# Zeros in the padded columns of two kinds of exponential tiles, written by ScalarE in place of GpSimd

## The chip, the core and the metric

The kernel runs on one core of a Trainium2 chip. The metric is the device time of one execution in microseconds (us). The core's engines are named as the profile names them: PE (TensorE, with PEld for its weight loads), DVE (VectorE), ACT (ScalarE), POOL (GpSimd) and SP (SyncE, which issues the large transfers). Each engine takes its instructions from its own queue, in the order in which the program wrote them.

## The reference, cut to what matters

An induced attention is followed by a soft mixture of experts, all in float32.

```python
def mab(q, kv):                       # B, N, m, C = 4, 11456, 32, 128
    s = scale * (q @ kv.transpose(0, 2, 1))
    s = s - s.max(-1, keepdims=True)
    a = np.exp(s)
    a /= a.sum(-1, keepdims=True) + 1e-09
    return a @ kv
h = mab(I, x)                         # 32 inducing points attend to x
x = mab(x, h).reshape(B * N, C)       # x attends to them
logits = x @ phi                      # 45824 x 32 slots
d = np.exp(logits - logits.max(0, keepdims=True))
d /= d.sum(0, keepdims=True) + 1e-9
slot_input = (d.T @ x).reshape(E, S_per_e, D)     # E, S_per_e, D = 8, 4, 128
slot_out[e] = np.maximum(slot_input[e] @ w1[e], 0.0) @ w2[e]   # hidden size 1024
c = np.exp(logits - logits.max(1, keepdims=True))
c /= c.sum(1, keepdims=True) + 1e-9
return c @ slot_out
```

## The kernel before, in words

Each of the 4 batches has 11456 rows of x, laid out as 90 blocks of 128 rows. A batch is cut into 6 tiles, five of 16 blocks and one of 10, so there are 24 tiles, and 12 pairs of them. Scores are kept as 32 rows (inducing points or slots) by four groups of 32 rows of x per block. In the last block of a batch only 64 rows are real. In the turned layout this leaves 16 columns of padding at the end of each batch's last tile: `valid(n)` is `width(n) - 16` there.

Stages, for each batch: the tiles of x are loaded (`xn`, and for most a transposed copy `xt`); the scores against the inducing points are formed pair by pair (`s`), their running maximum is taken, ACT writes the exponentials into `et` (L357, with a sum of the row), they are transposed (L369 on DVE, or L378 on PE with a copy back) and multiplied with `xn` (L393). After a batch's three pairs `group_fin` forms h. Then for each tile of that batch (`group_b`) follow the second attention (`s2p`, `bt`, `a`) and the logits (`lp`, kept in `l_all`). Three tiles make a segment (`group_seg`): the maximum over the segment (L780, L788, L791), the exponentials `dt` of its three tiles (L802, with the row sums in `z_l`), their transposes `d` (L808 on DVE, or PE and a copy), and the product with `a` into `u` (L818).

When all eight segments stand, `group_mlp` joins them: weights for the segments (`wl`, L864 and L903), the sum `zw` (L868), zeroed tiles `ma` and `mb` (g0: L952, and L954 twice), a matrix `wsel` of segment weights within `mb` (L877, POOL), its spreading over the partitions by PE (`wr`, L882), a weighted sum of the `u` (L885, L889, DVE), the expert inputs `sip` and `sit` (L894, L942), the last addition into `z1s` within `ma` (L957), the hidden layer (`hpm`, L967), its transposes (`htm` L980, with DVE copies L985), the second layer (`so`, L996) and its spreading (L1003, L1006, L1009). Fills (L231) are matmuls on zeros that keep PE at work. Then the outputs: each tile's row sums `zp` (L1106), the product `po` (L1125), evictions into `ot` by DVE, ACT or ACT with POOL (L1146, L1148, L1151, L1155), and stores (L1175). The softmax over slots for the outputs, the c-tiles, is done in between: maximum L1066 and its spreading L1070 on DVE, subtraction L1074 on POOL, exponential L1077 on ACT.

Every operation is recorded in a list with an engine, a cost and its dependences, and the list `ORDER` of operation numbers, written out by hand or by a planner beforehand, sets in which order they are issued. The costs given to `op` do not enter that order here; it stands in the code. Semaphore waits come from the buffers: `RINGS` gives `et` one buffer and `dt` two. The second buffer of `dt` that tile 23 takes was tile 21's before.

The padding of the exponentials has to be zero, since it is transposed and multiplied with the rest. The exponential writes the first `v` columns, and a second instruction, belonging to the same recorded operation, writes zeros to the other 16:

```python
nc.scalar.activation(et[:, :v], T["s1", p][:, :v], AF.Exp, ..., accum_out=zsum)   # L357
if v < w:
    nc.gpsimd.memset(et[:, v:w], 0.0)                                             # L359
```

The same is done for `dt` at L802 to L804. This happens for four pairs (2, 5, 8, 11) and four tiles (5, 11, 17, 23): eight memsets of 128x16 in all. `wz` (L226) is a constant 128x128 tile of zeros that DVE fills at the start and that the fills read.

Of the kernel before, what the change touches and what calls it, by code (L numbers as in the profile page):

```python
# [100 lines left out]
def width(n):  # L101
    return SIZES[n % NCH] * S


def seg_of(n):

    k = max(k for k in range(NSEG) if SEG_AT[k] <= n)
    return k, n - SEG_AT[k]
# [6 lines left out]
def valid(n):  # L115
    return width(n) - (PADS if n % NCH == NCH - 1 else 0)
# [24 lines left out]
class Plan:  # L141
# [6 lines left out]
    def op(self, eng, cost, name, fn, reads=(), writes=(), allocs=(), ni=0, uses=()):  # L148
        self.ops.append([eng, cost, name, fn, reads, writes, allocs, ni, uses])
# [3 lines left out]
def tile_kernel(ctx, tc, xn, xt_d, ind_t, phi, w1, w2, consts, out):  # L153
    nc = tc.nc
# [11 lines left out]
    def wtile(tag, key, n=JM * S):  # L166
        T[key] = work.tile([P, n], F32, tag=tag, name="_".join(map(str, key)), bufs=RINGS[tag])
        return T[key]

    def stile(tag, key, n=1, bufs=8):  # L170
        T[key] = small.tile([P, n], F32, tag=tag, name="_".join(map(str, key)), bufs=bufs)
        return T[key]

    def ptile(tag, key):
        T[key] = (pools[-1] if tag in ("sa", "sb") else ps).tile([P, 512], F32, tag=tag, name="_".join(map(str, key)), bufs=RINGS[tag])
        return T[key]
# [49 lines left out]
    wz = const.tile([P, P], F32, name="wz")  # L226
# [6 lines left out]
    def tiles_of(four):  # L233
        return [slice(32 * g, 32 * g + 32) for g in range(4)] if four else [slice(0, P)]

    def l_of(n):
        o = STARTS[n % NCH] * S
        return l_all[:, n // NCH, o : o + width(n)]

    def pe_turn(src_key, src, n, dst_tag, dst_key, prio, extra=(), virt=()):  # L240

        tk = ("tt", dst_key)
        dst = [(dst_tag, dst_key)]

        def tr():
            if virt:
                wtile(dst_tag, dst_key)
            pt = ptile("mm", tk)
            for q in range(4):
                nc.tensor.transpose(pt[:, q * P : (q + 1) * P], src()[:, q * P : (q + 1) * P], ident)  # L250

        def ev():
            nc.scalar.copy(T[dst_key] if virt else wtile(dst_tag, dst_key), T[tk])

        plan.op("PE", 0.48, prio, tr, [src_key, *extra], [tk], [("mm", tk), *((v, tk) for v in virt), *(dst if virt else ())], ni=8)
        plan.op("ACT", 0.48, prio, ev, [tk], [dst_key], [] if virt else dst)
# [59 lines left out]
    def group_pair(p):  # L316
# [3 lines left out]
        w, v = 512 + width(a1), 512 + valid(a1)  # L320

        def pr(op):
            return a1, op
# [29 lines left out]
        def aex():  # L353
            et = wtile("et", ("et", p), 1024)
            t = stile(hk[0], hk, P + 2, 2)
            zsum = T["hz", b][:, P + 1 :] if apart else t[:, P : P + 1]
            nc.scalar.activation(et[:, :v], T["s1", p][:, :v], AF.Exp, bias=T["negm1", b][:, c : c + 1], accum_out=zsum)  # L357
            if v < w:
                nc.gpsimd.memset(et[:, v:w], 0.0)  # L359

        def e_of(a):
            o = 512 * (a % 2)
# [46 lines left out]
        hk = ("hs", p) if c else ("hz", b)  # L409
# [8 lines left out]
        op = plan.op  # L418
        prev = [("ng", p - 1)] if c else []
        both = [("s1", a0), ("s1", a1)]  # L420
# [4 lines left out]
            op("ACT", 0.38 if c else 0.19, pr("am5"), am5, [("m1", p), *prev], [("m5", p)], [("m5", ("m5", p))])  # L425
        op("PE", 0.22, pr("apm"), apm, [("m5", p)], [("pm", p)], [("mm", ("pm", p))], ni=16 if p in CP else 4)
        op("DVE", 0.07, pr("ang"), ang, [("pm", p)], [("ng", p)])
        op("ACT", 0.24 + w / 1200, pr("aex"), aex, [*both, ("ng", p)], [("et", p), hk, ("zc", p)], [("et", ("et", p)), (hk[0], hk)], uses=[("s1", p)])
        if c:
            op("ACT", 0.19, pr("aal"), aal, [("ng", p), *prev], [("al", p)], [("al", ("al", p))])  # L430
            op("ACT" if p in HM else "Pool", 0.26 if p in HM else 0.4, pr("aal"), ahm, [("al", p)], [("hz", b)])
# [232 lines left out]
    def a2_of(n):  # L664
        return T["a2", n][:, : width(n)]
# [93 lines left out]
    def negm_of(k):  # L759

        k += k == NSEG - 1
        return negm_l[:, k : k + 1]

    def group_seg(k):
        op = plan.op
        seg = SEGS[k]
        ns = range(SEG_AT[k], SEG_AT[k] + seg)
        b = ns[0] // NCH
        last = ns[-1]

        def pr(o, n=last):
            return n, "B", o

        def h1():
            m4 = stile("m4b", ("m4b", k), SEG * 4)[:, : seg * 4]
            if HS[k] == "A":
                for i in range(seg):
                    nc.scalar.mul(m4[:, 4 * i : 4 * i + 4], mask4, T["mx2", k][:, i : i + 1])
                return
            (nc.vector if HS[k] == "D" else nc.gpsimd).tensor_tensor(  # L780
                m4.rearrange("p (i g) -> p i g", g=4), T["mx2", k][:, :seg].unsqueeze(2).broadcast_to([P, seg, 4]),
                mask4.unsqueeze(1).broadcast_to([P, seg, 4]), op=ALU.mult,
            )

        def h2():
            pmb = ptile("mm", ("pmb", k))
            for r in tiles_of(k in CH):
                nc.tensor.matmul(pmb[r, : seg * 4], rep[:, r], T["m4b", k][:, : seg * 4], start=True, stop=True)  # L788

        def h3():  # L790
            nc.vector.tensor_reduce(negm_of(k), T["pmb", k][:, : seg * 4], axis=AX.X, op=ALU.max, negate=True)  # L791

        op({"D": "DVE", "A": "ACT", "P": "Pool"}[HS[k]], {"D": 0.08, "A": 0.19 * seg, "P": 0.25}[HS[k]], pr("bch"), h1, [("mx2", n) for n in ns], [("m4b", k)], [("m4b", ("m4b", k))])
        op("PE", 0.22, pr("bch"), h2, [("m4b", k)], [("pmb", k)], [("mm", ("pmb", k))], ni=16 if k in CH else 4)
        op("DVE", 0.08, pr("bch"), h3, [("pmb", k)], [("ngl", k)])

        for i, n in enumerate(ns):

            def de(n=n, i=i):
                v = valid(n)  # L800
                dt_ = wtile("dt", ("dt", n))
                nc.scalar.activation(dt_[:, :v], l_of(n)[:, :v], AF.Exp, bias=negm_of(k), accum_out=z_l[:, k, i : i + 1])  # L802
                if v < width(n):
                    nc.gpsimd.memset(dt_[:, v : width(n)], 0.0)  # L804

            def td(n=n):
                w = width(n)
                nc.vector.transpose(wtile("d", ("d", n))[:, :w], T["dt", n][:, :w])  # L808

            def c2(n=n, i=i):  # L810

                if i == 0:
                    ptile("u", ("u", k))
                u, a2, d, nb = T["u", k], a2_of(n), T["d", n], SIZES[n % NCH]
                for j in range(nb):
                    q = slice(32 * (j % 4), 32 * (j % 4) + 32)
                    c = slice(j * S, j * S + S)
                    nc.tensor.matmul(u[q, :S], a2[:, c], d[:, c], start=i == 0 and j < 4, stop=i == seg - 1 and j >= nb - 4)  # L818

            w = width(n)  # L820
            op("ACT", 0.28 + w / 1200, pr("bde"), de, [("l", n), ("ngl", k)], [("dt", n), ("z", n)], [("dt", ("dt", n))])
            if n in TB:
                pe_turn(("dt", n), lambda n=n: T["dt", n], n, "d", ("d", n), pr("btd"))
            else:
                op("DVE", 0.07 + w / 960, pr("btd"), td, [("dt", n)], [("d", n)], [("d", ("d", n))])
            op("PE", 0.02 + 0.28 * w / 512, pr("c2"), c2, [("d", n), ("a2", n)], [("u", k)], [("u", ("u", k))] if i == 0 else [], ni=w // 8)

        if k < NSEG - 1:

            def u1():  # L830
                nc.scalar.copy(us_all[:, k * S : (k + 1) * S], T["u", k][:, :S])

            op("ACT", 0.16, pr("uf"), u1, [("u", k)], [("us", k)])
# [367 lines left out]
    for a in range(NT):  # L1201
        group_a(a)
        if a % 2:
            group_pair(a // 2)
        if a % NCH == NCH - 1:
            b = a // NCH
            group_fin(b)
            for n in range(b * NCH, (b + 1) * NCH):
                group_b(n)
                k, i = seg_of(n)  # L1210
                if i == SEGS[k] - 1:
                    group_seg(k)
# [89 lines left out]
```

## Time and profile before

| | |
|---|---|
| time, median of 3 runs | 228.7 us (228.14 to 229.79) |
| the profiled execution's own time | 228.22 us |
| its span in the profile | 226.4 us |
| mean granted clock of TensorE | 0.959 |
| PE / DVE busy | 202.7 us (90%) / 175.8 us (78%) |
| POOL / ACT busy | 130.3 us (58%) / 128.0 us (57%) |
| moved by DMA | 75.01 MB, mean 331 GB/s |

Times in the rows are microseconds from the start of the span. A busy PE is one whose pipeline holds matmuls; its ends are modelled. The granted clock is a share of 2.4 GHz. A row of a timeline gives start, duration, engine, line, operation, output and inputs, and in brackets how long the engine was idle before it and which instruction ended that.

### The profile page before, as it was taken

How to read it: one execution, taken by the hardware profiler on the slowest of the kernel's cores; microseconds unless marked ns; L12 is line 12 of the kernel's file. 1: busy time of each engine (PE TensorE's matmuls, PEld its weight loads, DVE VectorE, ACT ScalarE, POOL GpSimd, SP SyncE). 2: the span in 40 equal slices, each digit the busy share in tenths (PEclk: the TensorE clock that was granted, in tenths of full speed). 3: DMA queues.
4: the chain of work that ended last, by engine and by line, in shares of the span. 5: the costliest groups of instructions: out<-in, count | busy, mean ns of one | idle time of the engine just before them, and what ended most of it. 6: DMA issues, size and time to landing. Idle time of an engine off the chain costs nothing.

```text
span 226.4 us, 8096 instructions
## 1 busy us (share of the span) xinstructions
PE 202.7 (90%) x3370; PEld 141.9 (63%) x3370; DVE 175.8 (78%) x410; ACT 128.0 (57%) x339; POOL 130.3 (58%) x170
## 2 busy tenths in 40 slices
PE   8887899999999999999999998699999999899820
PEld 8664563546454663556654686598888878787710
DVE  0065548899899999999999998478898989868520
ACT  2463344563356676567764775133386699866730
POOL 0000105694537897588889982834669696867530
PEclk9999999999999999999999999659999999999975
DMA  6999998999999999999999900000099999999992
GB/s 225 402 428 417 428 420 323 377 427 419 400 376 389 414 388 360 410 389 419 387 412 427 395 14 0 3 3 3 28 408 403 403 395 419 393 421 421 404 408 89
DMA packets 14004, 75.01 MB, mean 331 GB/s; under 512 B 1808, under 2 KB 2448, under 8 KB 6928
## 3 DMA queue, kind: packets, MB, share of 16 engines
q1 hardware_dynamic: 13536, 74.32, 81.0%
q8 instruction: 26, 0.43, 0.7%
q10 hardware_dynamic: 432, 0.18, 0.3%
q14 instruction: 10, 0.08, 0.1%
HBM read 50.91 MB, written 23.59 MB: 329 GB/s over the span
## 4 chain that ended last, share of the span: by engine, by line
PE 55%; DVE 14%; DMA 13%; ACT 6%; issue 5%; POOL 3%; POOLq 0%; SPq 0%; ACTq 0%; DVEq 0%
PE po L1125 8%; PE zp L1106 7%; PE s L462 6%; DMA xt<-xt 5%; DMA xn<-xn 5%; PE ha L393 5%; PE s2p L462 4%; PE lp L715 4%; DMA l_all<-xt 3%; PE warm L231 2%; PE hpm L967 2%; DVE m L326 2%; PE u L818 2%; PE tp L290 2%; DVE bm L578 2%
## 5 line engine op out<-in xcount | busy, mean ns | idle before, releaser
L1155 POOL TENSOR_TENSOR ot<-ot,rzo 128x512 f32<-128x512 f32 (+1 forms) x26 | 25.9, 1006 | 15.6 <-ACT ot L1148 13.7
L1074 POOL TENSOR_TENSOR cs<-l_all,cs 128x512 f32<-128x512 f32 (+1 forms) x24 | 28.7, 1206 | 9.1 <-DVE cs L1070 9.1
L1125 PE MATMUL po<-mb,l_all 32*128 32x128 f32 x704 | 29.8, 285 | 1.7 <-ACT ot L1151 0.7
L1146 DVE TENSOR_TENSOR ot<-po,rzo 128x512 f32<-128x512 f32 (+1 forms) x48 | 28.3, 622 | 1.7 <-PE po L1125 1.4
L1151 ACT ACTIVATE ot<-po,rzo 128x128 f32<-128x128 f32 x85 | 24.1, 380 | 8.5 <-PE po L1125 7.2
L600 POOL TENSOR_TENSOR bt<-bt,bm 128x512 f32<-128x512 f32 (+1 forms) x21 | 20.6, 987 | 13.5 <-DVE bm L578 12.0
L1125 PEld LDWEIGHTS po<-mb,l_all 32*128 32x128 f32 x704 | 24.6, 186 | 5.7 <-DVE ot L1146 1.2
L690 POOL TENSOR_TENSOR a<-bt,bz 128x512 f32<-128x512 f32 (+1 forms) x24 | 23.7, 994 | 5.6 <-DVE bz L626 3.8
L1106 PE MATMUL zp<-cst,l_all 128*128 128x128 f32 x176 | 25.9, 287 | 0.9 <-DVE rzo L1114 0.6
L1106 PEld LDWEIGHTS zp<-cst,l_all 128*128 128x128 f32 x176 | 21.5, 190 | 4.4 <-issue 1.2
L715 PE MATMUL lp<-a2t,bdg 128*128 128x512 f32 (+1 forms) x48 | 23.6, 594 | 0.0
L393 PE MATMUL ha<-xn,e 128*32 128x128 f32 x668 | 21.9, 274 | 0.4 <-DMA xn<-xn 0.4
L393 PEld LDWEIGHTS ha<-xn,e 128*32 128x32 f32 x668 | 18.2, 110 | 3.8 <-issue 1.7
L617 POOL TENSOR_TENSOR hbuf<-bt 128x256 f32<-128x256 f32 (+1 forms) x24 | 16.7, 698 | 6.7 <-ACT bt L609 6.6
L357 ACT ACTIVATE et<-s,negm 128x1024 f32<-128x1024 f32 (+1 forms) x12 | 12.7, 1057 | 13.8 <-DVE negm L351 13.0
L462 PE MATMUL s<-xt,it_sb 128*32 128x512 f32 (+1 forms) x152 | 18.1, 571 | 2.6 <-ACT et L357 1.5
L802 ACT ACTIVATE dt<-l_all,negm_l 128x512 f32<-128x512 f32 (+1 forms) x24 | 16.6, 693 | 5.6 <-DVE negm_l L791 4.3
L462 PE MATMUL s2p<-xt,hts 128*32 128x512 f32 (+1 forms) x152 | 18.4, 574 | 0.2 <-ACT hts L491 0.2
L1148 ACT COPY ot<-po 128x512 f32<-128x512 f32 (+1 forms) x26 | 14.4, 580 | 4.7 <-PE po L1129 1.9
L609 ACT ACTIVATE bt<-bt 128x512 f32<-128x512 f32 (+1 forms) x23 | 13.6, 600 | 5.3 <-POOL bt L600 3.1
L1077 ACT ACTIVATE l_all<-cs 128x512 f32<-128x512 f32 (+1 forms) x24 | 14.1, 616 | 4.0 <-POOL cs L1074 4.0
L326 DVE TENSOR_REDUCE m<-s 128x1 f32<-128x1024 f32 (+1 forms) x12 | 13.6, 1136 | 2.1 <-PE s L462 2.0
(187 smaller groups left out, 390.7 us busy)
## 6 DMA issues: line engine op xcount, KB each, us to landing
xn<-xn SPq DMA_DIRECT2D x18, 1024.0 KB, 11.3
xt<-xt SPq DMA_DIRECT2D x13, 1024.0 KB, 10.1
out<-ot SPq DMA_DIRECT2D x12, 1024.0 KB, 6.9
w<-w SPq DMA_DIRECT2D x8, 1024.0 KB, 9.8
out<-ot SPq DMA_DIRECT2D x10, 512.0 KB, 6.3
l_all<-xt SPq DMA_DIRECT2D x3, 1024.0 KB, 7.2
out<-ot SPq DMA_DIRECT2D x12, 256.0 KB, 2.9
xt<-xt SPq DMA_DIRECT2D x3, 640.0 KB, 10.3
```

Source lines behind the costliest of these rows:

```text
L326: nc.vector.tensor_reduce(stile("m1", ("m1", p)), T["s1", p][:, :v], axis=AX.X, op=ALU.max)
L393: nc.tensor.matmul(ha[32 * q : 32 * q + 32, :P], e[:, j * S : (j + 1) * S], T["xn", a][:, j * P : (j + 1) * P], start=a == a0 and j < 4, s ...
L462: nc.tensor.matmul(dst[32 * g : 32 * g + 32, :w], lhs, src, start=True, stop=True)
L600: nc.gpsimd.tensor_tensor(tv, tv, mb(), op=ALU.subtract)
L690: nc.gpsimd.tensor_tensor(blocks(a2), blocks(t), zb, op=ALU.mult)
L715: nc.tensor.matmul(lp[r, :w], T["bdg", b][:, r], T["a2t", n][:, :w], start=True, stop=True)
L1074: nc.gpsimd.tensor_tensor(t, l_of(n), t, op=ALU.subtract)
L1106: nc.tensor.matmul(zp[:, q * P : (q + 1) * P], e[:, q * P : (q + 1) * P], mask4s, start=True, stop=True, skip_group_check=True)
L1125: nc.tensor.matmul(T[po[g]][:, q * P : (q + 1) * P], e[r, q * P : (q + 1) * P], T["srs",][r, :], start=True, stop=True, skip_group_check=True)
L1146: nc.vector.tensor_tensor(dst, src, parts(g)[1], op=ALU.mult)
L1151: nc.scalar.mul(dst[:, q], src[:, q], T["rzo", n][:, g + 4 * q : g + 4 * q + 1])
L1155: nc.gpsimd.tensor_tensor(dst, dst, z, op=ALU.mult)
```

## The change

The two memsets are replaced by ACT copies of as many columns of `wz`. Two costs in the recorded operations are raised by 0.09 to account for them; the list `ORDER` is the same, so each copy stands in ACT's queue right behind the exponential whose tile it completes.

```diff
             nc.scalar.activation(et[:, :v], T["s1", p][:, :v], AF.Exp, bias=T["negm1", b][:, c : c + 1], accum_out=zsum)
             if v < w:
-                nc.gpsimd.memset(et[:, v:w], 0.0)
+                nc.scalar.copy(et[:, v:w], wz[:, : w - v])
...
-        op("ACT", 0.24 + w / 1200, pr("aex"), aex, ...
+        op("ACT", (0.33 if v < w else 0.24) + w / 1200, pr("aex"), aex, ...
...
                 nc.scalar.activation(dt_[:, :v], l_of(n)[:, :v], AF.Exp, bias=negm_of(k), accum_out=z_l[:, k, i : i + 1])
                 if v < width(n):
-                    nc.gpsimd.memset(dt_[:, v : width(n)], 0.0)
+                    nc.scalar.copy(dt_[:, v : width(n)], wz[:, : width(n) - v])
...
-            op("ACT", 0.28 + w / 1200, pr("bde"), de, ...
+            op("ACT", (0.37 if valid(n) < w else 0.28) + w / 1200, pr("bde"), de, ...
```

The first place is POOL's queue where the slots of the last segment end and the expert network begins. `dt_2299` is the tile `dt` of tile 23, `a_21_2180` an operand of the last segment, `ma` and `mb` the tiles that g0 zeroes, and `cs` the c-tiles; a wait names the engine or the transfer queue whose semaphore is waited for.

```order
 L690 TENSOR_TENSOR a_21_2180<-bt_2008,bz_2147 128x512 [waits DVE_49,PE_49]
 L868 TENSOR_TENSOR zw<-wl,z_l 128x21 [waits Activation_49]
-L804 MEMSET dt_2299 128x16 [waits DVE_49]
 L952 MEMSET ma 128x288 [waits DMAHW7_49,DMAHW5_49]
 L954 MEMSET ma 128x1152
 L954 MEMSET mb 128x1152 [waits DMAHW3_49,DMAHW2_49]
 L877 TENSOR_TENSOR mb<-cst,wl 128x224
-L1074 TENSOR_TENSOR cs_2263<-l_all,cs_2263 128x512
+L1074 TENSOR_TENSOR cs_2263<-l_all,cs_2263 128x512 [waits DVE_49]
 L1074 TENSOR_TENSOR cs_1701<-l_all,cs_1701 128x512
```

The memset and its wait for DVE have left POOL's queue; L952 follows L868, and the first c-tile now carries a wait for DVE of its own.

The second place is ACT's queue at the same point of the program; `us_all` is the copy of segment 6's `u`, and `wl` and the next line's instructions are the weights of the last segment.

```order
 L831 COPY us_all<-u_2188 128x32 [waits PE_49]
 L802 ACTIVATE dt_2299,z_l<-l_all,negm_l 128x304 [waits DVE_49]
+L804 COPY dt_2299<-wz 128x16
 L903 ACTIVATE wl_2360<-negm_l,nm 128x2 [waits DVE_49]
 L921 ACTIVATE ws_2362<-cst,wl_2360 32x32 [waits Activation_49]
```

The copy came in between the exponential of tile 23, whose wait for DVE covers the same buffer, and L903; it has no wait.

The third place is ACT's queue at pair 2, the last pair of batch 0; `hs_269` is the copy of the product `ha` of the pair before, which POOL adds up at L416.

```order
 L401 ACTIVATE al_290<-negm_0_214 128x1
 L357 ACTIVATE et_329,hz_223<-s_2_292,negm_0_214 128x816 [waits DVE_49,Activation_49]
+L359 COPY et_329<-wz 128x16
 L413 COPY hs_269<-ha_305 128x128 [waits PE_49]
 L401 ACTIVATE al_370<-negm_0_214 128x1
```

Here the copy stands ahead of L413. The queues of PE and SP are the same in both kernels; on DVE the order is the same, and the transposes of the padded tiles no longer wait for POOL.

## Rows read from the trace of the kernel before

**Rows 1.** Page: DMA share in 40 slices; below, busy time by stretch, granted clock.
```profile
DMA  6999998999999999999999900000099999999992
...
core 0: us, PE busy (x) PEld busy (x) DVE busy (x) ACT busy (x) POOL busy (x), PEclk, DMA share, GB/s
16.00:18.00 2.00, 1.00 (x9) 0.52 (x13) 0.58 (x2) 1.90 (x4) 0.00 (x0) 1.00 1.00 422
...
136.00:140.50 4.50, 4.44 (x58) 3.45 (x57) 3.85 (x13) 2.27 (x6) 0.13 (x1) 1.00 0.00 0
140.50:143.50 3.00, 0.00 (x0) 0.00 (x0) 1.20 (x3) 1.44 (x6) 2.96 (x6) 0.88 0.00 0
143.50:153.00 9.50, 9.47 (x164) 8.28 (x168) 6.67 (x15) 1.96 (x6) 4.95 (x5) 0.50 0.01 3
153.00:161.00 8.00, 7.97 (x216) 6.91 (x207) 7.09 (x18) 2.74 (x6) 4.11 (x4) 1.00 0.01 2
...
170.00:200.00 30.00, 29.08 (x493) 24.81 (x487) 26.85 (x65) 24.59 (x74) 24.44 (x24) 1.00 0.99 404
```

**Rows 2.** The chain that ended last: start, duration, what (four of its pieces).
```profile
34.36 7.18 DMA l_all<-xt
...
136.13 4.40 issue
...
149.86 5.19 PE hpm L967 x128
...
155.79 3.84 PE so L996 x128
```

**Rows 3.** Timeline of POOL, 128 to 146 us.
```profile
135.90 0.23 POOL L868 TENSOR_TENSOR zw<-wl,z_l 128x21 f32<-128x21 f32 x1 [0.71 <-ACT dt L802]
140.54 0.11 POOL L804 MEMSET dt<- 128x16 f32 x1 [4.42 <-DVE nm L900]
...
143.43 2.50 POOL L1074 TENSOR_TENSOR cs<-l_all,cs 128x512 f32<-128x512 f32 x2
```

**Rows 4.** Timeline of PE, 128 to 152 us.
```profile
137.61 0.61 PE L231 MATMUL fill<-wz 128*128 128x128 f32 x4
...
139.99 0.46 PE L818 MATMUL u<-d,a 128*32 128x32 f32 x32
143.53 1.11 PE L882 MATMUL wr<-mb,ones 32*128 32x224 f32 x2 [3.08 <-POOL mb L877]
...
146.50 1.92 PE L894 MATMUL sip<-mb,h 128*128 128x32 f32 x8
...
148.66 1.20 PE L231 MATMUL fill<-wz 128*128 128x128 f32 x4
```

**Rows 5.** Timeline of DVE, 128 to 172 us.
```profile
140.47 0.71 DVE L808 STREAM_TRANSPOSE d<-dt 128x512 f32<-128x512 f32 x1
141.34 0.51 DVE L808 STREAM_TRANSPOSE d<-dt 128x320 f32<-128x320 f32 x1 [0.15 <-ACT dt L802]
144.68 0.39 DVE L885 TENSOR_TENSOR mb<-us_all,wr 128x224 f32<-128x224 f32 x1 [2.83 <-PE wr L882]
145.10 0.95 DVE L889 TENSOR_TENSOR mb<-mb 128x96 f32<-128x96 f32 x1
...
149.05 0.19 DVE L957 TENSOR_TENSOR ma<-sit,sis 128x32 f32<-128x32 f32 x1 [0.19 <-DVE sis L930]
...
155.35 0.29 DVE L985 COPY ma<-htm 128x128 f32<-128x128 f32 x1 [0.84 <-PE htm L980]
```

**Rows 6.** ACT's small instructions: L734 by line, then the timeline at 27 us.
```profile
L734 ACT COPY l_all<-lp x2: 157/165/173, 103.5 to 122.8; 128x16 f32<-128x16 f32 x2
...
27.73 0.26 ACT L413 COPY hs<-ha 128x128 f32<-128x128 f32 x1
27.88 0.30 ACT L401 ACTIVATE al<-negm 128x1 f32<-128x1 f32 x1
```

**Rows 7.** One line of DVE with two SBUF inputs: durations min/median/max in ns.
```profile
L333 DVE SCALAR_TENSOR_TENSOR m<-cst,m,m x8: 221/223/645, 20.9 to 105.4; 128x4 f32<-128x4 f32 x8
```

More of the change, by code (lines that the diff above doesn't have):

```diff
@@ L427, in group_pair @@
         op("DVE", 0.07, pr("ang"), ang, [("pm", p)], [("ng", p)])
-        op("ACT", 0.24 + w / 1200, pr("aex"), aex, [*both, ("ng", p)], [("et", p), hk, ("zc", p)], [("et", ("et", p)), (hk[0], hk)], uses=[("s1", p)])
+        op("ACT", (0.33 if v < w else 0.24) + w / 1200, pr("aex"), aex, [*both, ("ng", p)], [("et", p), hk, ("zc", p)], [("et", ("et", p)), (hk[0], hk)], uses=[("s1", p)])
         if c:
@@ L820, in group_seg @@
             w = width(n)
-            op("ACT", 0.28 + w / 1200, pr("bde"), de, [("l", n), ("ngl", k)], [("dt", n), ("z", n)], [("dt", ("dt", n))])
+            op("ACT", (0.37 if valid(n) < w else 0.28) + w / 1200, pr("bde"), de, [("l", n), ("ngl", k)], [("dt", n), ("z", n)], [("dt", ("dt", n))])
             if n in TB:
```

## The prediction

> **What bounds the kernel now.** I read the DMA line of the page first, then the busy time by stretch. In slices of 5.66 us, loads fill the DMA engines up to the 23rd, about 130 us, and stores fill them again from the 30th, about 164 us, on; DMA share is 0.99 in 170 to 200 [rows 1]. Between the two nothing is transferred and the kernel waits on its own dependences: the last slot exponentials, then the small expert network. There one stretch stands out. In 140.5 to 143.5 TensorE is busy 0.00 us of 3.00, with DVE and ACT under half, while POOL works 2.96; and from 143.5 to 153 the granted clock is 0.50 [rows 1]. The chain of waits says the same: a piece of 4.40 us "issue" from 136.13, work of nobody [rows 2]. The timeline of POOL names it: after `zw` (L868, ended 135.90 + 0.23 = 136.13) POOL stands 4.42 us in front of the memset L804, put down to DVE [rows 3]. That memset writes the padding of the last tile `dt`, tile 23. The ring `dt` has two buffers, so it may write only when the transpose of tile 21 has read the same buffer. Queued behind it on POOL are the three memsets of g0, the product L877 (`wsel`), and the c-tiles L1074; none of these needs tile 23. TensorE's L882 needs L877, and its row shows 3.08 us idle on POOL L877 [rows 4].
>
> **The wait on POOL goes.** In the change L952 stands right behind L868. Its own waits are for transfers of tiles long since used, and 0.00 of DMA share is left in 136 to 140.5 [rows 1], so it starts at 136.13. From L952 to the end of L877 POOL needs 143.48 - 140.65 = 2.83 us, taking the end of L877 as the start of L882 less 0.05 [rows 3, 4]. L877 then ends near 139.0. L882 is no longer held by it but by TensorE itself, busy with L818 until 139.99 + 0.46 = 140.45. It starts 143.53 - 140.45 = **3.1 us earlier**.
>
> **What is late next.** The matmuls L818 of tiles 22 and 23 wait for DVE's transposes, ending at 140.47 + 0.71 = 141.18 and at 141.34 + 0.51 = 141.85 [rows 5]. The latter now also waits for the new ScalarE copy. Taken at 0.2 us (below), 142.05. So TensorE has work from 140.45 to 141.0 (L882, at about half of its 1.11), to 141.2 a gap, then L818, with a second short gap to 142.05, done near 142.3, and L924 near 142.7. I see no gap above 0.3 us.
>
> **The clock.** After the 3.08 us gap the clock went to 0.50, the 1.2 GHz level, and came back to 1.00, 2.4 GHz, only at about 153. Work done in between can be priced at the full level: four fills take 1.20 us at 148.66 and 0.61 at 137.61 [rows 4]; the 128 matmuls L967 take 5.19 us, mostly at 0.50, and the 128 of L996 with the same shapes 3.84 at 1.00 [rows 2]. The smaller L894 (1.92 us) I take at the fills' ratio, 1.0. Will it stay at 1.00 once the gap is gone? In 16 to 18 us TensorE is busy only 1.00 of 2.00 us and the clock stays 1.00 [rows 1]; the gaps left here are shorter. I take it that it stays.
>
> The sum along this path: L894 needs DVE's L889, which took 0.95 us [rows 5]. That is no time of a 96-column sum: L957 takes 0.19 for 32 columns. It stood beside POOL's two L1074 (143.43 + 2.50 = 145.93) and ended 0.12 after them. L333 shows the same pair of times, 223 ns typical and 645 at most [rows 7]. In the change these L1074 come after L877 and after their DVE operand, about 139.5 to 142.0, so L889 runs undisturbed: L885 from 142.05 (0.39), L889 about 0.2, done 142.65. L894 starts at 142.7 in place of 146.50, 3.8 us earlier, and ends near 143.8. From its end to the end of L957 was 149.24 - 148.42 = 0.82 (the fills at 148.66 began when L942 was nearly done); L957 thus starts near 144.4 in place of 149.05: **4.6 earlier**. L967 and its 128 matmuls at full clock would give 1.3 us more. But DVE, in program order, has the c-tiles behind L957: from 149.24 to 154.51 (155.35 less the 0.84 idle before it [rows 5]) it is full, 5.3 us. So L985 starts near 149.9 in place of 155.35: **5.45 us earlier**, bound by DVE now. From there the same rows follow in the same order, and stores keep the DMA engines full from the first one on, so the end moves as far as the first store does.
>
> In the Trainium skill, GPSIMD Engine Reference, section 1, the SBUF interfaces are shared with VectorE, with contention for its instructions that have two SBUF inputs. By that rule L889 (both inputs in `mb`) is held and L885, whose `wr` is in PSUM, is not; the trace agrees, 0.95 against 0.39 us. Were the lengthening no contention, L889 would keep 0.95 and the gain would shrink by 0.75 at most.
>
> **The copies added on ScalarE.** Eight copies of 128x16 replace eight memsets. No row shows one that reads SBUF: the nearest are the 128x16 copy from PSUM, 0.157 to 0.173 us (L734), and a one-column activation from SBUF, 0.30 (L401) [rows 6]. I take 0.2 in the queue; consecutive small ones overlap, so 0.1 is possible, and 0.3 the upper bound. Seven of the eight stand before 130 us, where loads bind. One lies on the chain: behind the exponential of pair 2, at 27.8 us, the copy delays L413, POOL's sum, the fin of batch 0 and so the load issued at 34.36 [rows 2, 6]. This costs **0.2 us** (0.1 to 0.3). The others are followed by work that waits for POOL, DVE or loads, with ACT half idle; all on the path they would add 7 x 0.3 = 2.1. The seven other memsets are 0.11 us of POOL each, as the eighth [rows 3]; POOL is the releaser of little in that stage, so their removal I count at nothing, 0.8 us at best. The eighth, tile 23, is in the path above. L903 and L921 behind it are hidden by L818.
>
> **Sum.** -5.45 + 0.2 = -5.25 against the profiled execution, 228.22: 222.97. The median of the runs shown is 228.7, 0.5 above it, so **223.4**.
>
> **Rivals.** (a) The clock falls all the same. Then TensorE's rows from L882 on keep their length and move by the 3.08 alone: -3.08 + 0.2 = -2.9, 225.8. For it: the short gaps that remain, and that L818 and L924 are small work. Against it: 16 to 18 us. TensorE: Matmul & The Clock Gate, in the Trainium skill (A second HAM failure mode: psum-queue depth-cycling), has frequent micro-idles between groups of matmuls making the clock oscillate; it would give this 225.8. The rows at 16 to 18 speak against it for gaps of this length. (b) The gain is used up within 2.3 us. The 5.3 us of c-tiles on DVE would have to be slower because POOL's L1074 meet them at another time, or stores find their first tile late: 226.4 to 228.7, say 227.5. Against: every engine is idle at about 142.5 [rows 1, 4, 5], so nothing there needs the time. (c) Slower: the seven copies before 130 us each hold ACT where something on the loads' path is behind them, at 0.3 us each: +2.1, 230.8. It decides only if less than 2.1 of the gain behind 136 arrives at the end. Against: ACT is busy 2.27 of 4.50 and 1.44 of 3.00 us [rows 1], and only the copy of pair 2 has a piece of the chain right behind it. (d) The change does not do what it says: L952 takes the memset's place as what waits on POOL, for a release that the rows don't show. +0.2, 228.9. Against: L952 began at once when the memset was done, and its waits are for transfers.
>
> **How the numbers follow.** Forecast 0.58 (its own range 222.3 to 224.6: bounds of L889, of the copies and of the DVE block), (a) 0.26, (b) 0.10, (c) 0.03, (d) 0.03. The range 222.3 to 226.1 takes in the forecast and (a). One per cent, about what a measurement tells here, is 2.3 us: below 226.4 lies all of the forecast and all of (a), 0.84; (b) and (d) give 0.13 within; (c) makes 0.03 slower.
>
> **What would show it.** In the profile after: no idle on POOL before L952, and L868 to L952 without a gap; L882 near 140.6; no 3 us hole of TensorE and 1.00 of clock through 140 to 153; L889 near 0.2 us; L967 near 3.9; DVE without idle before L985, or under 0.3 us; stores that fill the DMA engines from about 158.5 in place of 164; the end 5 us earlier behind the same length of stores. I am wrong if the clock stays at 0.50 behind L882, if POOL waits at L952, or if loads end later than 130 us by more than 0.5.

## The result, and the profile after

The changed kernel takes **222.4 us** (median of 4 runs, 222.03 to 223.09); the kernel before, on the same chip and beside it, 228.9 us (4 runs, 228.14 to 229.79). The ratio is 0.972, with an interval from 0.968 to 0.976: 6.5 us faster (5.5 to 7.4). A second comparison, with more runs (e5 below), gives 0.979 (0.974 to 0.983), about 5 us less. What both intervals allow is 5.5 to 5.9 us. Medians and ratios leave out executions in a slower state, and the profile of one run, e2, was taken in it, so that only the tail of that profile is read.

| | before | after |
|---|---|---|
| profiled execution's own time | 228.22 us | 222.03 us |
| its span | 226.4 us | 220.2 us |
| mean granted clock | 0.959 | 0.983 |

The page of after, the line of the DMA share in 40 slices (now of 5.5 us), and below it the busy time by stretch, cut as in [rows 1] from 136 to 161:

```profile
DMA  6999998999999998999999950000499999999992
...
136.00:140.50 4.50, 4.50 (x64) 3.44 (x65) 3.98 (x12) 2.75 (x8) 3.90 (x5) 1.00 0.00 0
140.50:143.50 3.00, 2.77 (x99) 2.55 (x99) 2.58 (x9) 1.53 (x9) 1.90 (x2) 1.00 0.02 5
143.50:153.00 9.50, 8.39 (x256) 7.39 (x259) 9.17 (x20) 3.84 (x9) 3.98 (x4) 1.00 0.01 3
153.00:161.00 8.00, 8.00 (x142) 7.01 (x134) 7.17 (x18) 4.40 (x12) 5.29 (x6) 1.00 0.45 172
```

The gap without transfers is about one slice shorter and the stores begin within 153 to 161. TensorE's empty 3 us are gone (2.77 busy of 3.00), and the granted clock is 1.00, 2.4 GHz, where it was 0.50, 1.2 GHz. The timeline of POOL after, to be laid beside [rows 3]:

```profile
135.40 0.23 POOL L868 TENSOR_TENSOR zw<-wl,z_l 128x21 f32<-128x21 f32 x1 [0.71 <-ACT dt L802]
135.57 0.34 POOL L952 MEMSET ma<- 128x288 f32 x1
...
137.87 0.56 POOL L877 TENSOR_TENSOR mb<-cst,wl 128x224 f32<-128x224 f32 x1
139.03 2.52 POOL L1074 TENSOR_TENSOR cs<-l_all,cs 128x512 f32<-128x512 f32 x2 [0.60 <-DVE cs L1070]
```

L952 has no bracket: no idle time stands between it and L868. The timeline of PE after, for [rows 4]:

```profile
139.88 0.64 PE L882 MATMUL wr<-mb,ones 32*128 32x224 f32 x2
140.45 0.76 PE L818 MATMUL u<-d,a 128*32 128x32 f32 x64
141.44 0.38 PE L818 MATMUL u<-d,a 128*32 128x32 f32 x20 [0.23 <-DVE d L808]
141.75 0.43 PE L924 MATMUL wr<-ws,ones 32*128 32x64 f32 x2
142.11 1.08 PE L894 MATMUL sip<-mb,h 128*128 128x32 f32 x8
...
144.07 3.70 PE L967 MATMUL hpm<-w,ma 128*32 128x128 f32 x128
147.70 0.33 PE L980 MATMUL htm<-cst,ma 128*128 128x128 f32 x1
```

L882 follows other matmuls without a wait, and the largest gap between it and the end of the hidden layer (L967) is 0.23 us. The timeline of DVE after, for [rows 5]:

```profile
140.87 0.51 DVE L808 STREAM_TRANSPOSE d<-dt 128x320 f32<-128x320 f32 x1 [0.18 <-ACT dt L804]
141.31 0.35 DVE L885 TENSOR_TENSOR mb<-us_all,wr 128x224 f32<-128x224 f32 x1
141.69 0.26 DVE L889 TENSOR_TENSOR mb<-mb 128x96 f32<-128x96 f32 x1
...
143.82 0.19 DVE L957 TENSOR_TENSOR ma<-sit,sis 128x32 f32<-128x32 f32 x1 [0.19 <-DVE sis L930]
...
147.54 1.11 DVE L912 SCALAR_TENSOR_TENSOR zl<-zl,wl,zs 128x1 f32<-128x1 f32 x1
148.57 0.70 DVE L1070 STREAM_TRANSPOSE cs<-cm 128x512 f32<-128x512 f32 x1
149.20 0.25 DVE L985 COPY ma<-htm 128x128 f32<-128x128 f32 x1
```

The wait for ScalarE's copy is the 0.18 us in front of L808; before, the same transpose waited 0.15 for the exponential [rows 5], and it starts 5.47 us behind L868 in place of 5.44. L985 begins without idle time, although its operand, the first L980, ended at about 148.0: DVE is late here, not TensorE.

**How the runs are compared from here.** The start of L868 scatters between executions of one kernel, between 134.4 and 137.8 us where nothing was added in front of it (139.8 in e2's profile); behind the first L985 all is rigid (71.0 us from its start to the end of the span, in before, in after and in the experiments). So each profile is read by T, from the start of L868 to the start of the first L985, cut at L882 (TensorE's first step of the network) and L957 (what the hidden layer waits for). The columns are differences of the starts in those rows, in us.

| kernel | L868 to L882 | L882 to L957 | L957 to L985 | T |
|---|---|---|---|---|
| before | 7.63 | 5.52 | 6.30 | 19.45 |
| after | 4.48 | 3.94 | 5.38 | 13.80 |
| e1, tile 23 alone | 4.48 | 3.94 | 5.38 | 13.80 |
| e2, the other seven alone | 7.63 | 5.51 | 6.30 | 19.44 |
| e3, memset moved on POOL | 4.48 | 4.52 | 5.37 | 14.37 |
| e4, hole filled | 7.63 | 3.50 | 5.39 | 16.52 |
| e5, after once more | 4.53 | 3.94 | 5.40 | 13.87 |
| e6, POOL late by two memsets | 5.20 | 3.50 | 5.40 | 14.10 |
| e7, POOL late by four memsets | 7.43 | 3.84 | 6.95 | 18.22 |
| e8, one DVE step earlier | 4.47 | 3.95 | 4.45 | 12.87 |
| e9, copies five times | 4.44 | 3.94 | 5.38 | 13.76 |

The change takes 5.65 us out of T: 3.15, 1.58 and 0.92. In e1 and e2 lines behind L804 are numbered 3 higher, in e9 lines behind the copies 1 or 2 higher.

### The profile page after: what moved, and what is told of

Its sections match the earlier page's. It is cut to its first block, busy times and chain, and to the rows that moved or that the text cites. A ratio compares the mean times of both kernels' runs of the same rounds, so it can differ in the third digit from the quotient of the medians.

```text
span 220.2 us, 8093 instructions
## 1 busy us (share of the span) xinstructions
PE 198.2 (90%) x3370; PEld 137.6 (62%) x3370; DVE 175.3 (80%) x410; ACT 129.4 (59%) x347; POOL 129.9 (59%) x162
## 4 chain that ended last, share of the span: by engine, by line
PE 46%; DVE 32%; ACT 7%; issue 4%; POOL 3%; DMA 2%; POOLq 0%; SPq 0%; DVEq 0%; ACTq 0%
PE po L1125 9%; PE zp L1106 8%; DVE m L326 5%; PE s L462 5%; PE lp L715 4%; PE ha L393 4%; PE s2p L462 4%; DVE bt L570 3%; DVE bm L578 3%; DVE d L808 3%; DVE a2t L710 3%; DMA xn<-xn 2%; DVE cs L1070 2%; ACT et L357 2%; PE u L818 2%
## 5 line engine op out<-in xcount | busy, mean ns | idle before, releaser
L1074 POOL TENSOR_TENSOR cs<-l_all,cs 128x512 f32<-128x512 f32 (+1 forms) x24 | 28.8, 1208 | 7.8 <-DVE cs L1070 7.8
L407 POOL TENSOR_TENSOR hz<-hz,al 128x129 f32<-128x129 f32 x7 | 2.8, 399 | 22.6 <-ACT al L401 22.4
```

The source lines that it names most:

```text
L1074: nc.gpsimd.tensor_tensor(t, l_of(n), t, op=ALU.subtract)
```

## The experiments

Theory: all of the gain is tile 23's memset, which held POOL; the wait it caused and the clock that fell in TensorE's gap each have a part of it. Rivals: the seven other replacements matter, for better or (rival c) worse; ScalarE as the writer matters, not the place in POOL's queue; the clock falls by itself.

**Tile 23 alone (e1) and the other seven alone (e2).** The edits, against the kernel before; e2 has the two arms the other way round, and ScalarE's copy at L359:

```diff
-                    nc.gpsimd.memset(dt_[:, v : width(n)], 0.0)
+                    if n == NT - 1:
+                        nc.scalar.copy(dt_[:, v : width(n)], wz[:, : width(n) - v])
+                    else:
+                        nc.gpsimd.memset(dt_[:, v : width(n)], 0.0)
```

> Only the zeros of tile 23 are written by ACT; the other seven memsets stay on POOL. Theory (the wait of this one memset on POOL is everything behind 136 us): POOL goes from L868 to L952 without a gap, L882 starts near 140.4, the clock stays at 1.00, the time is 222.4 to 222.9. If the 0.5 us by which the front part of the changed kernel was early (L868 at 135.40 in place of 135.90) comes from the seven others, it is 222.9 and L868 is at 135.9; if that was chance, 222.4. Rival (the seven others share in the gain by freeing POOL in the load stage): 224 to 227.

> The seven other zeros are written by ACT, that of tile 23 stays a memset on POOL. Theory: the wait of 4.4 us on POOL, the idle 3.1 us of PE and the clock of 0.50 are all there again, 228.9 (228.4 if the front part's 0.5 us is real, 229.1 if the copies cost the 0.2 us that was forecast). Rival (the gain is shared): 224 to 227. Copies that delay the loads: up to 231.

e1 measured 223.6 us, ratio 0.982 (0.976 to 0.987). e2: 228.1 us, ratio 1.000 (0.997 to 1.003). e1's T is that of after in each of its parts; its median is some 0.7 us above what was expected, and the tail is not the cause: in its profile L868 started at 136.92, 1.5 later than in after, and TensorE stood before two late loads there, which in after it didn't:

```profile
102.58 1.60 PE L462 MATMUL s<-xt,it_sb 128*32 128x512 f32 x16 [0.66 <-DMA xt<-xt]
...
108.38 1.08 PE L393 MATMUL ha<-xn,e 128*32 128x128 f32 x32 [0.95 <-DMA xn<-xn]
```

POOL in e2:

```profile
139.80 0.23 POOL L871 TENSOR_TENSOR zw<-wl,z_l 128x21 f32<-128x21 f32 x1 [0.72 <-ACT dt L802]
144.44 0.11 POOL L805 MEMSET dt<- 128x16 f32 x1 [4.41 <-DVE nm L903]
```

The wait of 4.41 us is there as in [rows 3], and T is 19.44. So the 5.65 us are tile 23's, and the seven others together are worth nothing that the times can tell (0.8 us either way).

**The memset stays on POOL, behind L877 (e3).** All eight memsets are POOL's; tile 23's exponential records its memset no more. The memset is issued behind L877 (operation 726), in front of the first c-tile, and DVE's transpose of that tile (operation 702) is issued behind it:

```diff
-                if v < width(n):
+                if v < width(n) and n < NT - 1:
...
+            if i == 702:
+                continue
...
+            if i == 726:
+                nc.gpsimd.memset(T["dt", NT - 1][:, valid(NT - 1) : width(NT - 1)], 0.0)
+                plan.ops[702][3]()
```

> All eight memsets stay on POOL, but that of tile 23 stands behind the product L877 and not in front of L952. Theory (it is the place in POOL's queue, not the engine): L882 near 140.4 again and a clock of 1.00, but POOL's two L1074 now wait behind the memset until 140.5 and run 140.6 to 143.1, beside DVE's L889, which takes near 1 us again; so 0.5 to 0.8 us slower than the changed kernel, 222.9 to 223.4. Rival (the engine matters): 228.9.

It measured 222.3 us (of three executions), ratio 0.977 (0.971 to 0.983), the same as after within the intervals. L882 comes at the same 4.48. The engine that writes the zeros is not what counts; what stands behind the write in the queue is. T is 0.57 longer than after's, as expected, and these rows of POOL, DVE and PE say why:

```profile
139.25 2.50 POOL L1074 TENSOR_TENSOR cs<-l_all,cs 128x512 f32<-128x512 f32 x2
...
140.80 1.07 DVE L889 TENSOR_TENSOR mb<-mb 128x96 f32<-128x96 f32 x1
...
141.93 1.08 PE L894 MATMUL sip<-mb,h 128*128 128x32 f32 x8 [0.64 <-DVE mb L889]
```

L889 came while POOL worked on the second of two L1074, which ended at 141.75, and ended 0.12 us after it. In after it began at 141.69, when L1074 had just ended (139.03 + 2.52 = 141.55), and took 0.26.

**The hole filled, the wait left (e4).** Before, with 12 matmuls on zeros between L818 and L882, nothing else changed:

```diff
+            if i == 727:
+                warm(("fill1",), 12)
```

> The kernel before with twelve more matmuls on zeros on PE between L818 and L882, about 2.7 us, so that PE works through the wait on POOL, which stays at 4.4 us. Theory (wait and clock each have a part): the clock stays at 1.00, L882 still at 143.5, then L894 near 146.1 since L889 is still held by POOL's L1074, L967 starts 1.5 and L985 about 2.1 us earlier than before: 226.5 to 227. Rival (the clock costs nothing, the wait everything): 228.9. Rival (the clock is everything): 223.

225.3 us, ratio 0.990 (0.986 to 0.994). POOL waits as before and L882 comes 7.63 after L868 as before; the clock is 1.00 from 130 to 160. PE (which records each of the 12 twice), then DVE:

```profile
138.92 2.94 PE L231 MATMUL fill<-wz 128*128 128x128 f32 x24
142.07 0.64 PE L882 MATMUL wr<-mb,ones 32*128 32x224 f32 x2 [0.21 <-POOL mb L877]
...
143.50 0.43 PE L924 MATMUL wr<-ws,ones 32*128 32x64 f32 x2
143.87 1.08 PE L894 MATMUL sip<-mb,h 128*128 128x32 f32 x8
...
143.18 0.26 DVE L889 TENSOR_TENSOR mb<-mb 128x96 f32<-128x96 f32 x1
```

T is 2.93 shorter than before's. I had expected 2.1, with L889 held by POOL as before; but here it came at the moment at which the first L1074 (from 141.97, about 1.25 us) ended, and passed before the next. Part of the 2.93 hangs on that. Held for 0.95 again, L889 would have ended at 144.13 and L894, which began at 143.87 behind TensorE's own L924, would have come some 0.3 us later; held to the end of the second L1074, some 0.7. In before the hold delayed nothing: L889 ended at 146.05, and L894 began at 146.50 behind L924 [rows 4, 5]. So the lost clock cost 2.2 to 2.9 us, and the wait itself, 19.45 - 13.80 less these, 2.7 to 3.4.

**The changed kernel once more (e5).** No edit; it is what the runs below are compared with.

> The changed kernel once more, beside the kernel before on this chip. The stretch from the start of L868 to the start of the first L985 was 19.45 us before and 13.80 after; it should be 13.80 again. If the start of L868 (135.90 before, 135.40 after, 134.4 to 136.9 in the fast profiles of the experiments so far) only scatters from execution to execution, the gain is 5.65 us, a ratio of 0.975; if the seven other copies help the load stage, 6.5 us, 0.972, and L868 is at 135.4 or earlier.

222.7 us (222.11 to 224.28), ratio 0.979 (0.974 to 0.983). T is 13.87. The tail repeats within 0.07, and the 6.5 us of the first comparison was partly chance in front of L868.

The times beside the experiments show another spread, of the kernel before itself. The mean granted clock of its 53 executions there is either 0.958 to 0.960 (28 of them) or 0.964 to 0.967 (25), and those of the second kind are 0.7 to 1.6 us shorter in the mean on the three chips used. The profile of before (0.959) is of the first kind, so its T of 19.45, and with it the 5.65 us, stands for the longer kind; of the other no profile was taken.

**POOL late without any wait (e6, e7).** The changed kernel, with two or four more memsets of 1152 columns in front of L877:

```diff
+            if i == 721:
+                for _ in range(4):
+                    nc.gpsimd.memset(T["z2",][0], 0.0)
```

> The changed kernel with two more memsets of 1152 columns on POOL between L954 and L877, so that L877 ends 2.1 us later. Theory: 1.4 of it are slack, since PE works until 139.9; L882 starts 0.7 late behind a short idle gap, the clock stays at 1.00; from L868 to L985 14.4 to 14.6 us in place of 13.80, so 0.6 to 0.8 us slower than the changed kernel. Rival (PE's path has no slack, or any new gap drops the clock): 2.1 to 4 us slower.

> The same with four memsets, L877 4.2 us later without any wait for tile 23. Theory: L882 starts behind 2.8 us of idle PE, the clock drops to 0.50 as before, from L868 to L985 19.0 to 19.3 us, so 5.2 to 5.5 us slower than the changed kernel, nearly the time before. If the clock holds through this gap: 16.4 to 16.7, 2.7 slower, as where the gap was filled. Rival (the memset's wait for tile 23 mattered in another way than by POOL's lateness): no more than 2 us slower.

e6: 223.5 us, ratio 0.981 (0.976 to 0.987). e7: 228.1 us, ratio 1.003 (0.999 to 1.006). With four, the whole gain is gone, though ScalarE writes the zeros and nothing on POOL waits for tile 23: that L877 is late is cause enough. Both expected values of T were too high. In e6 the 2.17 us of POOL became 0.65 us of idle time of TensorE, and T is only 0.30 longer than after's, where 0.6 to 0.8 was expected. The rows of DVE and PE show why:

```profile
143.25 0.51 DVE L808 STREAM_TRANSPOSE d<-dt 128x320 f32<-128x320 f32 x1 [0.19 <-ACT dt L804]
143.69 0.35 DVE L885 TENSOR_TENSOR mb<-us_all,wr 128x224 f32<-128x224 f32 x1
...
144.77 1.08 PE L894 MATMUL sip<-mb,h 128*128 128x32 f32 x8
```

L885 starts 5.91 us behind L868, exactly as in after: DVE's transposes stand in front of it in both, so L882 had 0.7 us more slack than I had counted. Only L894 came later, 6.99 in place of 6.71, behind TensorE's L818 and L924. In e7, where 19.0 to 19.3 was expected, the clock fell later than in before and L889 wasn't held by POOL (0.26); the parts of the two aren't separated. PE and DVE of e7, and its stretches:

```profile
143.75 0.64 PE L882 MATMUL wr<-mb,ones 32*128 32x224 f32 x2 [2.88 <-POOL mb L877]
...
148.33 5.92 PE L967 MATMUL hpm<-w,ma 128*32 128x128 f32 x128
...
154.54 0.29 DVE L985 COPY ma<-htm 128x128 f32<-128x128 f32 x1 [1.51 <-PE htm L980]
...
140.50:143.75 3.25, 0.37 (x33) 0.26 (x33) 1.61 (x4) 1.91 (x9) 3.13 (x5) 1.00 0.00 0
143.75:146.00 2.25, 2.25 (x92) 1.86 (x93) 1.27 (x6) 0.19 (x1) 2.25 (x2) 1.00 0.03 7
146.00:153.00 7.00, 7.00 (x104) 6.45 (x107) 6.17 (x12) 2.05 (x6) 3.56 (x4) 0.51 0.01 2
```

After an idle 2.88 us TensorE started again at 1.00, and fell to 0.51 only at about 146, while it was busy 2.25 of 2.25. The part up to L957 is thus short (3.84), the part behind it long (6.95): the 128 matmuls L967 take 5.92 in place of 3.70, and DVE waits 1.51 for TensorE. After the 0.65 of e6 the clock stays at 1.00. This profile's mean granted clock is 0.968; of e7's ten executions four have 0.965 to 0.968 and six 0.959 or 0.960, so it doesn't stand for all of them.

**What bounds the tail now (e8).** DVE does, by the rows of after; so the changed kernel with L912, operation 743, recorded right behind L957 instead of behind six c-tile instructions:

```diff
-        for i in ORDER:
+        order = [i for i in ORDER if i != 743]
+        order.insert(order.index(740) + 1, 743)
+        for i in order:
```

> The changed kernel with L912, a DVE instruction on one column, right behind L957 and not behind the four c-tiles. In the changed kernel it takes 1.11 us beside POOL's L1074 and DVE is full from L957 to L985. Theory (it is held by POOL's running instruction): it takes 0.2 us where POOL is idle, L985 comes 0.9 us earlier, when L980 is done; from L868 to L985 12.8 to 13.0, so 0.9 us faster than the changed kernel, 221.5. Rival (the 1.1 us are its own): no change.

**221.3 us** (220.21 to 222.28), ratio 0.972 (0.967 to 0.976) where the change, beside it, has 0.979: faster than both kernels. T is 12.87, 0.93 less than after's; the medians are 1.4 apart. DVE of e8:

```profile
144.26 0.21 DVE L912 SCALAR_TENSOR_TENSOR zl<-zl,wl,zs 128x1 f32<-128x1 f32 x1
...
148.60 0.25 DVE L985 COPY ma<-htm 128x128 f32<-128x128 f32 x1
```

One column took 1.11 us in after, from 147.54 to 148.65, beside two L1074 of POOL that ran from 146.12 to 148.64; here POOL was idle and it took 0.21. The gain of 0.90 went through to the first L985 whole: in after DVE binds that stretch.

**The copies in front (e9).** The changed kernel with each of the seven copies before 130 us issued five times; a repeat waits for the one before it, so five take 1.14 us in place of 0.19.

```diff
-                nc.scalar.copy(et[:, v:w], wz[:, : w - v])
+                for _ in range(5):
+                    nc.scalar.copy(et[:, v:w], wz[:, : w - v])
...
-                    nc.scalar.copy(dt_[:, v : width(n)], wz[:, : width(n) - v])
+                    for _ in range(1 if n == NT - 1 else 5):
+                        nc.scalar.copy(dt_[:, v : width(n)], wz[:, : width(n) - v])
```

> The change with each of the seven copies before 130 us issued five times (four pairs' L359, three tiles' L804), tile 23's once. Each repeat adds some 0.2 us of ScalarE, so +0.8 to 0.9 us at each of seven places. Theory: only pair 2's copy has a piece of the chain right behind it, so the start of L868 moves by about +0.8 to 0.9 beside the change and the median by as much, to about 223.5; from L868 to L985 nothing changes (13.8). Rival c, all seven on the path of the loads: +5.6 to 6, about 228.5. If none is on the path: as the change, about 222.7.

227.3 us, ratio 0.999 (0.996 to 1.001): 4.6 us over the change (0.999 against 0.979 of some 228), near rival c and far from my theory. T is untouched; L868 starts at 140.19 in place of 135.40. Laid side by side, the starts of ScalarE's exponentials show where the 4.8 us come in: 0.93 behind pair 2, 0.64 behind pair 5 (0.73 beside e5 and e8), 0.31 and 0.33 behind pair 8 and tile 5, 0.95 behind pair 11, 0.87 behind tile 11 and 0.69 behind tile 17, of 0.95 added at each. The waits on ScalarE in its trace (PE's weight load behind pair 11, then DVE and PE behind tile 11):

```profile
109.39 1.14 ACT L360 COPY et<-wz 128x16 f32<-128x16 f32 x5
...
110.31 0.14 PEld L379 LDWEIGHTS tt<-cst,et 128*128 128x128 f32 x1 [0.24 <-ACT et L360]
...
117.18 0.51 DVE L810 STREAM_TRANSPOSE d<-dt 128x320 f32<-128x320 f32 x1 [0.90 <-ACT dt L806]
...
117.29 1.06 PE L463 MATMUL s2p<-xt,hts 128*32 128x512 f32 x8 [0.78 <-ACT hts L492]
```

So each of the seven places has a piece of the path close behind it, at five of them with some 0.3 us or less to spare. That the change itself didn't lose 2.1 us there is a matter of the copies' size, not of their places. By the same starts a single copy, in after, e5 and e8 against e1, e3 and e4 (which write those zeros on POOL), costs 0.11 at pair 2 (11.70 us to the next exponential, against 11.59), 0.10 at pair 11 (1.03 against 0.93), and nothing at pair 5 in e5 and e8 and at tiles 5, 11 and 17. At pair 8 the spread among kernels with the same code is as large as a difference could be, and that place stays open.

## Why the prediction was right, and where its steps were not

**The wait on POOL, right.** L952 follows L868 with no idle time. L882 was put 4.55 us behind L868 (140.45 against 135.90) and comes 4.48 behind it; e1 and e2 show that this is tile 23's memset alone, e7 that POOL's lateness suffices without it.

**What is late next, right.** I saw no gap of TensorE above 0.3 us; there is one of 0.23, behind the transpose that waits 0.18 for the copy. The 0.2 that I added there for the copy was too much: the transpose is 0.03 later behind L868 than before. L903 and L921 behind that copy delay nothing: L924, which needs L921, ends right where L894 begins.

**The clock, right.** It is 1.00 from 136 to 161. Rival a is thus out, and its price was about right: forecast 2.35 us less gain than the likeliest case, measured 2.2 to 2.9 by e4. Gaps of 0.23 (after) and 0.65 (e6) left the clock at 1.00. One argument against rival b was misread: "every engine is idle at about 142.5" isn't so, since POOL works 2.96 of the 3.00 us there [rows 1].

**L889, right, though with little to spare.** 0.26 us, forecast about 0.2. It found POOL free by 0.14 us; e3 shows what it costs where it doesn't, 0.81. The 0.75 that the gain could shrink by if L889 kept its 0.95 was about right: T of e3 is 0.57 longer. In before itself the long L889 delayed nothing, since L894 stood behind L924 there. GPSIMD Engine Reference, section 1, in the Trainium skill, has contention for VectorE's instructions with two SBUF inputs on the interfaces shared with GpSimd. The traces agree, by L889 (1.07 beside POOL, 0.26 apart) and by L912 (1.11 and 0.21).

**The DVE block, right.** L957 was put 8.5 us behind L868 and comes 8.42 behind it; L985 14.0 and 13.80. The block of c-tiles between them was taken from before as 5.3 us and is 5.19 (149.20 less 144.01). That DVE binds there is shown by e8. I did not see that the block held a stall of its own, L912's 0.9 us.

**The copies, right in the sum and wrong in the reason.** One copy takes 0.192 us (192/192/193 ns for the four of L359), and the timeline of ScalarE in after shows what it adds:

```profile
27.63 0.19 ACT L359 COPY et<-wz 128x16 f32<-128x16 f32 x1
27.72 0.27 ACT L413 COPY hs<-ha 128x128 f32<-128x128 f32 x1
```

L413 starts 0.09 after the copy. ScalarE: Activation LUTs, in the Trainium skill (What ACT_TABLE_LOAD costs), gives 186 ns and 0.833 ns a column for an ACTIVATE with immediate scale and bias, by an estimate 199 ns for 16 columns, and an overlap of 93 ns between ACTIVATEs back to back; the rows agree, 0.192 and 0.10. I had put 0.2 at pair 2 alone; it is 0.11 there and 0.10 at pair 11. The step that failed is "seven of the eight stand before 130 us, where loads bind". The loads do fill the DMA engines, but the dependences between the engines are as tight. The chain that ended last has three loads in before (7.18, 10.71 and 12.01 us), in after only the first at the start (5.37), and in e9 none among its 195 longest pieces. And the shares of ACT that I held against rival c are of 136 to 143.5, where none of the seven copies stands. In the busy time by stretch DVE works all but 0.2 of 10 us, with DMA share at 0.95 to 0.99; the same stretch of before and of after:

```profile
120.00:130.00 10.00, 9.98 (x185) 5.97 (x185) 9.81 (x28) 6.30 (x17) 9.54 (x14) 1.00 0.99 414
```

```profile
120.00:130.00 10.00, 9.98 (x188) 6.41 (x188) 9.79 (x29) 6.23 (x19) 9.54 (x13) 1.00 0.95 396
```

Rival c's mechanism is real: at 0.1 us a copy it costs 0.2 in all, at 1.14 us a place it takes the whole gain.

**The sum.** -5.45 was forecast for T, -5.65 measured; +0.2 for the front, about +0.2 measured. The 5.45 us in all lie just under the 5.5 to 5.9 that both comparisons allow. The median, 1.0 below the 223.4, is 0.2 T's and for the rest in front of L868, which in the two profiles starts 0.50 apart (135.90 and 135.40). Two waits there are of that size: in before's profile TensorE stood before two late loads, in after's it didn't. Before, and then the first of the two matmuls in after:

```profile
41.59 1.06 PE L462 MATMUL s<-l_all,it_sb 128*32 128x512 f32 x8 [0.55 <-DMA l_all<-xt]
...
57.50 0.85 PE L393 MATMUL ha<-xn,e 128*32 128x128 f32 x20 [0.38 <-DMA xn<-xn]
```

```profile
40.87 1.04 PE L462 MATMUL s<-l_all,it_sb 128*32 128x512 f32 x8
```

Such waits come and go between executions, whatever stands in front: the first is 0.96 in e6 and 0.52 in e2, and there is none in e1, e3 and e4, which have the memsets of before there. They are no part of the change. Whether they explain the medians too can't be read from one profile each, and what makes the loads late wasn't tried.

## What to carry to other kernels

An instruction of 0.1 us is dear where it waits in an in-order queue: look behind every small write for what stands there and doesn't need it, and move the write to where its wait is due anyway, on another engine or further back in the same queue (e1 and e3 gave the same time within their intervals). Price the gap that such a wait opens twice, once for its length and once for TensorE's clock behind it. And an edit "off the path" is one whose cover was measured: the seven copies were free or nearly so at 0.1 us, but not because their engine was half idle.

## What the runs showed of the hardware

**Two DVE instructions with two SBUF inputs end with POOL's.** L889 took 0.95 in before, 1.07 in e3 and 0.26 in after, e4, e6 and e7; L912 1.11 and 0.21. The long ones ended 0.01 to 0.12 us after the POOL TENSOR_TENSOR that was running when they came. In e4, e6 and e7 L889 came as the first of three L1074 ended and went through before the second was done: what counts is the POOL instruction under way, not that POOL has more behind it. A memset on POOL did not hold L780, which also has two SBUF inputs: it took 0.17 in after beside L954, and 0.17 in before with POOL idle. L885, with one input in PSUM, isn't held: it took 0.35 to 0.39 in all runs, and in e6 it came 0.81 us into an L1074 and was done before that one ended.

**The clock doesn't always fall in the gap.** In before's profile TensorE, idle for 3.08 us, came back at 0.50; in e7's, idle for 2.88, it came back at 1.00 and fell 2.2 us later, for about 7 us, in the middle of full work. Whoever looks only at the gap's own stretch sees no loss there. That the length of the gap decides between the two isn't shown: both kernels have executions with a mean granted clock near 0.96 and near 0.966, and one profile of each was taken.
